# Nystromformer attention with a multiplicative feed-forward layer: the same pieces of work in another hand-planned order

## The chip, the cores and the metric

The kernel runs on one core of one Trainium2 chip. The metric is device time in microseconds (us) from launch to the last output byte. The chip's engines work side by side, each through its own instructions strictly in program order: TensorE (PE, with PEld for its weight loads), VectorE (DVE), ScalarE (ACT), GpSimd (POOL) and SyncE (SP). SP and POOL also start the transfers of this kernel, so a transfer that must wait holds back whatever its engine has queued behind it.

## The reference, cut to what matters

There are 8 batches of 8 heads with 576 rows of 64 numbers. `q_lm` and `k_lm` are means over groups of 18 rows, 32 of them per head.

```
A  = softmax(q @ k_lm.T / 8)         # 576 x 32
Bm = softmax(q_lm @ k_lm.T / 8)      # 32 x 32
C  = softmax(q_lm @ k.T / 8)         # 32 x 576
Z  = Bm.T / (norm1(Bm) * norminf(Bm) + 1e-6)
for _ in range(6): Z = 2*Z - Z @ Bm @ Z
attn = A @ Z @ C @ v                 # per batch and head
x    = attn, heads side by side      # 4608 x 512
out  = ((x @ w1) * (x @ w2)) @ w3 @ w_out
```

## The kernel before

All work is cut into small pieces, each a function call, and a long text `ORDER` lists the pieces by hand. The program walks the list once and every piece issues its instructions on its engines at that moment. There is no scheduler behind it: each engine's queue is the order of the list. A token is a letter for the kind of piece and digits for batch (or pair of batches), half and so on.

The first third of the time is the fold. Since nothing lies between the last two matrices, w3 and w_out are multiplied once into `w34`, in 112 pieces `f` (line 564) after a Strassen-like scheme. Its left factors come from 16 row blocks of w3, each loaded by a token `l` on SP's queue (line 525) and turned by a token `t` on PE (four transposes through the one PSUM tile `pst`, line 540), then copied out by ACT or, for every block of the kind "21", read by three DVE subtractions (lines 550 to 552). T1 to T4 are four DVE sums over w_out (line 510).

While this goes on, attention begins. These are its pieces:

- `K` loads q or k of a batch on POOL's queue (line 99, converting to 16 bits), `W` loads half of v of a batch on SP's queue (line 114).
- `T` is the DMA transpose of a loaded q or k, on SP's queue (line 122). It waits for the load, and for the attention of two batches earlier to be done with the two buffers `qT` or `kT`.
- `P` and `Q` are the same transposition made on PE instead, for two heads at a time (line 138), for k of batches 0 and 1 and q of batch 0. They go through PSUM tile `ptt`, which shares the one buffer with `pst`. `P` copies the result out on ACT, `Q` on DVE (line 139). The twelve such pieces are the only ones.
- `L` and `M` make the group sums, `L` on POOL in four instructions (lines 195 to 200), `M` on DVE in one (line 190). `X` and `Y` join the two halves of the sums into `lmk` and `qbd`: `X` with four copies on ACT and three sums on POOL (lines 208 to 215), `Y` with all of it on DVE.
- `C` and `c` are the scores for matrix C (PE line 304, ACT exponential line 309, row sums on POOL for `C` and on DVE for `c`). `V` and `v` are C @ v (line 332), `A` is the scores for matrix A (PE line 350, ACT line 355), `S` and `N` are their normalisation (lines 364 to 384).
- `B`, `J`, `R`, `I` and `Z` are, for a pair of batches, the scores Bm, a chain of twelve small DVE operations, the residual and the six steps of the inverse, and the product with C @ v.
- `G` and `g` multiply by w1 or w2 (line 414) with the result taken out by ACT (`G`, line 420) or DVE (`g`, line 422). `w` loads w1 or w2 on POOL's queue into the space of turned w3 blocks (line 612), `E` copies a part of it to the upper partitions on DVE (line 617).
- `U` is an eighth of a batch's two products: two PSUM tiles of `big`, the first copied out by ACT (line 441), the second multiplied with it by DVE (line 442). `D` multiplies 128 rows by w34 (line 463); ACT takes the result out (line 467) and SP stores it (line 483).

PSUM is what couples the engines most. During the fold there is one `big` tile, two of `small`, one of `pst` and three of `psw`. After the last `f` all of this is given back and there are three of `big` and two of `small`:

```
    def end_of_fold():
        psf.release()
        pf.release()
        ...
        ps["big"] = 3
```

Of the kernel before, what the change touches and what calls it, by code (L numbers as in the profile page):

```python
# [16 lines left out]
D = 64  # L17
# [19 lines left out]


ORDER = """
l f l f l f t f t f T1 f f f f t f f f t l l f f T2 f f f T3 f f l f l f f t f f f f W00 f f f T4 f f  # L40
Pk03 f f Pk02 t f f f f Pk01 f Pk00 f f Pq01 f f Pq02 Kk2 f Pq03 f Pq00 f W10 f Pk11 f Mq00 f Mk00 Pk12
Mk01 f Pk13 Mq01 f Kq2 f t f Pk10 X0 W01 f Mk10 f t f f f t f c01 f t c00 Tq1 Mq10 f w0 Lk11 W11 f A00 f
f f v01 A01 f f f Mq11 f f S0 f X1 f f Tq2 f B0 A10 f l J0 f C11 t f f f E3 f Tk2 Kk3 f f R0 f l v11 t
I00 f Lq20 Mk20 w1 l f t A11 I01 f v00 E0 f E2 C10 Mk21 t S1 E1 E7 I02 f f f f Tk3 f f W30 f f f E5 f
Lq21 Kq3 f Tq3 Kk4 f f v10 I03 Lk30 E4 f f f f f I04 f f X2 I05 f E6 Z0 f f W20 f f G110 g010 G000 C20
Kq4 N01 W21 N00 G011 g001 Mq30 Lq31 G100 C21 U U Mk31 G101 U X3 v20 N10 N11 U A21 B1 Tk4 U U A20 C31 Kk5
U Lk40 U v21 G111 W31 C30 Tq4 J1 D U R1 U Kq5 v31 I10 A30 A31 S2 Tk5 Lq40 W40 Lk41 Tq5 Mq41 U D N21 I11
S3 X4 Lk50 N20 U D I12 U I13 U I14 A41 D Kq6 C41 Mq50 U I15 Kk6 W41 A40 V30 U N30 D Lq51 N31 Z1 Mk51 Tq6
D X5 g210 G310 g200 D A51 B2 G201 Kk7 S4 G311 G211 J2 D U c40 D U A50 R2 U Tk6 Kq7 I20 U U I21 G300 U
I22 C50 W50 U U v41 Lq60 Lq61 g301 I23 Mk60 C51 Mk61 Tk7 D W51 Tq7 U U X6 D N41 D U U I24 A60 v40 S5 U U  # L50
Lk70 v50 W60 Mq70 I25 U c60 D U Lk71 Lq71 X7 N40 V51 D N50 C61 W70 Z2 A61 B3 D J3 G410 G400 G500 W71 D
N51 R3 W61 g501 G401 I30 g411 G510 I31 U I32 U C71 D U U v61 G511 I33 U U D c70 A70 I34 U U v70 S6 U D U
A71 I35 V71 U U V60 U Z3 D N61 U U G610 S7 G700 g600 D N60 U g601 G611 D U U G710 g711 U U U D N70 U
g701 U D U N71 D U U D U D U D U D U D U D U D D D D D
"""

@with_exitstack
# [690 lines left out]
```

## Time and profile before

| what | value |
|---|---|
| median of 13 runs | 288.23 us (284.05 to 296.13) |
| the profiled execution's own time | 285.41 us |
| its span | 283.2 us |
| PE busy | 267.4 us, 94% |
| DVE busy | 179.1 us, 63% |
| ACT busy | 140.5 us, 50% |
| POOL busy | 102.8 us, 36% |
| fold ends, three `big` begin | about 90 us |
| last DMA transpose issued, landed | 170.2 us, 177.2 us |

The own time is 2.2 us more than the span, for what lies around it. The median of the runs is 2.8 us above the profiled execution. A PE instruction's busy time counts from its start to a modelled end, so consecutive ones overlap; where below a piece's own length on PE is needed, it is taken from start to start of neighbouring pieces.

### The profile page before, as it was taken

What the parts mean: (1) busy time and instruction counts of PE and PEld (TensorE: products, weight loads), DVE (VectorE), ACT (ScalarE), POOL (GpSimd) and SP (SyncE); (2) the same over time, 40 slices, a digit from 0 to 9 for tenths busy, and PEclk for the clock granted to TensorE, in tenths of its full rate; (3) what the DMA queues carried; (4) which work ended last, traced back from release to release, by engine and by line L of the source; (5) the groups of instructions that cost most, each with busy time, mean ns of one, the idle gap of its engine ahead of it and who ended that gap; (6) DMA issues with size and microseconds to landing.
All of it is one profiled execution on the core that took longest, in us unless ns stands there. A gap on an engine that the chain in (4) does not pass through costs nothing.

```text
span 283.2 us, 8838 instructions
## 1 busy us (share of the span) xinstructions
PE 267.4 (94%) x3765; PEld 182.5 (64%) x3765; DVE 179.1 (63%) x341; ACT 140.5 (50%) x243; POOL 102.8 (36%) x148
## 2 busy tenths in 40 slices
PE   6999999997999899899999999999999999999994
PEld 2787766775885577566546766765767755665552
DVE  1766359897975877796677585959447586642310
ACT  2212356531322787455496655577565466443431
POOL 0170216276477666975540299750200000000000
PEclk9999999999999999999999999999999999999999
DMA  6999999999999997999999999539311012123344
GB/s 184 355 321 237 220 176 112 209 202 195 172 196 200 193 217 130 153 206 180 262 201 173 159 159 223 151 76 264 93 28 40 23 39 74 37 76 79 88 109 137
DMA packets 60999, 44.94 MB, mean 159 GB/s; under 512 B 32544, under 2 KB 53536, under 8 KB 60960
## 3 DMA queue, kind: packets, MB, share of 16 engines
q1 hardware_dynamic: 46112, 31.70, 50.6%
q0 software_dynamic: 13632, 11.54, 29.0%
q10 hardware_dynamic: 1216, 1.15, 1.3%
q8 instruction: 29, 0.48, 0.8%
q14 instruction: 10, 0.08, 0.1%
HBM read 38.80 MB, written 9.44 MB: 170 GB/s over the span
## 4 chain that ended last, share of the span: by engine, by line
PE 77%; ACT 7%; DVE 5%; DMA 4%; POOL 2%; SPq 2%; issue 2%; ACTq 0%; POOLq 0%; DVEq 0%
PE small L463 20%; PE big L435 19%; PE psw L564 14%; PE small L283 4%; PE small L332 4%; PE big L414 4%; PE pst L540 2%; PE big L304 2%; DMA raw<-in_moe_w_dram 2%; DMA w3g<-in_moe_w_dram 2%; PE ptt L138 1%; SPq L122 1%; PE big L350 1%; ACT gt L420 1%; PE big L381 1%
## 5 line engine op out<-in xcount | busy, mean ns | idle before, releaser
L442 DVE TENSOR_TENSOR ab<-a_sb,big 128x576 f16<-128x576 f16 x64 | 48.1, 753 | 44.8 <-ACT a_sb L441 40.7
L435 PE MATMUL big<-ahat,gt 128*128 128x288 f16 x512 | 71.3, 286 | 0.2
L463 PE MATMUL small<-w,ab 128*128 128x512 f16 (+1 forms) x296 | 67.5, 374 | 0.0
L435 PEld LDWEIGHTS <-gt 128*128 128x128 f16 x512 | 48.3, 98 | 18.3 <-issue 2.4
L441 ACT CAST a_sb<-big 128x576 f16<-128x576 f32 x64 | 40.9, 638 | 14.4 <-PE big L435 13.9
L463 PEld LDWEIGHTS <-ab 128*128 128x128 f16 x296 | 27.9, 98 | 29.0 <-issue 2.1
L467 ACT ACTIVATE o_sb<-small 128x512 f32<-128x512 f32 (+1 forms) x36 | 21.4, 594 | 36.9 <-PE small L463 36.9
L420 ACT ACTIVATE gt<-big 128x1024 f16<-128x1024 f32 x21 | 20.8, 1029 | 7.5 <-PE big L414 7.5
L314 POOL TENSOR_TENSOR e<-ect 96x384 f32<-96x384 f32 x11 | 10.9, 993 | 30.5 <-ACT ect L309 28.9
L414 PE MATMUL big<-wdup,zt 128*32 128x512 f16 x256 | 17.2, 381 | 1.4 <-DVE w L573 0.5
L341 ACT ACTIVATE xd<-small,rcr 128x64 f32<-128x64 f32 x16 | 5.0, 313 | 25.0 <-DVE rcr L339 25.0
L564 PE MATMUL psw<-wof,s 128*128 128x256 f32 x64 | 16.9, 392 | 0.0
L564 PE MATMUL psw<-tmat,s 128*128 128x256 f32 x64 | 16.5, 390 | 0.2 <-DVE tmat L510 0.2
L309 ACT ACTIVATE ect<-big 96x768 f32<-96x768 f32 x16 | 12.9, 806 | 6.0 <-PE big L304 5.9
L283 PE MATMUL small<-sz 32*32 32x64 f32 (+1 forms) x768 | 14.8, 214 | 0.5 <-DVE sz L271 0.5
L283 PEld LDWEIGHTS small<-sz 32*32 32x32 f32 x768 | 11.1, 105 | 6.3 <-issue 4.0
L384 DVE TENSOR_TENSOR ahat<-eat,big 128x576 f16<-128x576 f16 x16 | 11.9, 751 | 5.1 <-PE big L381 5.0
L564 PE MATMUL psw<-wof,a 128*128 128x256 f32 x48 | 14.4, 413 | 0.2 <-ACT a L547 0.2
L422 DVE TENSOR_SCALAR gt<-big 128x1024 f16<-128x1024 f32 x11 | 13.4, 1221 | 1.8 <-PE big L414 1.8
L332 PE MATMUL small<-vt,ect 96*32 96x64 f32 x768 | 14.0, 221 | 0.0
L355 ACT ACTIVATE eat<-big 128x576 f16<-128x576 f32 x16 | 10.3, 649 | 6.9 <-PE big L350 6.3
L564 PEld LDWEIGHTS psw<-tmat,s 128*128 128x128 f32 x64 | 11.4, 190 | 2.4 <-DVE tmat L510 0.6
(128 smaller groups left out, 398.7 us busy)
## 6 DMA issues: line engine op xcount, KB each, us to landing
vt<-in_v_dram SPq DMA_DIRECT2D x16, 576.0 KB, 6.4
out_dram<-o_sb SPq DMA_DIRECT2D x23, 192.0 KB, 2.3
nat<-in_k_dram POOLq DMA_DIRECT2D x7, 576.0 KB, 8.7
nat<-in_q_dram POOLq DMA_DIRECT2D x7, 576.0 KB, 7.8
raw<-in_moe_w_dram SPq DMA_DIRECT2D x13, 256.0 KB, 6.7
out_dram<-o_sb SPq DMA_DIRECT2D x24, 128.0 KB, 2.6
wdup<-in_moe_w_dram POOLq DMA_DIRECT2D x2, 1024.0 KB, 11.9
out_dram<-o_sb SPq DMA_DIRECT2D x23, 64.0 KB, 2.3
```

The source lines that it names most:

```text
L283: nc.tensor.matmul(psI[sl, 64 * a:64 * a + n], src[sl, a, 32:64], src[sl, a, 0:n], start=True, stop=True, tile_position=(32 * h, 32 * h))
L309: nc.scalar.activation(out=ect.rearrange("p (j a) h m -> p h j a m", a=2), in_=flat[0:P, 0:768].rearrange("p (h j a m) -> p h j a m", j=JJ ...
L332: nc.tensor.matmul(psV[32 * h:32 * h + 32, 0:64], st["ect", qd][:, c, h, :], st["v"][:, 4 * qd + h, c, :], start=(c == 0), stop=(c == TK - 1),
L414: nc.tensor.matmul(psG[32 * h:32 * h + 32, n, :], st["zt"][h % 2][:, qd, h // 2, :], wdup[w][:, 4 * qd + h, 512 * n:512 * n + 512], start= ...
L420: nc.scalar.activation(out=dst, in_=src, func=AXF.Copy, scale=1.0 / ZS)
L422: nc.vector.tensor_scalar(out=dst, in0=src, scalar1=1.0 / ZS, scalar2=None, op0=ALU.mult)
L435: nc.tensor.matmul(p[:, c, 0:HS], st["g", qd][:, w, 128 * j:128 * j + 128], st["ahat", qd][:, c, :], start=(qd == 0), stop=(qd == 1))
L441: nc.scalar.copy(out=a_sb, in_=p[:, :, 0:HS])
L442: nc.vector.tensor_tensor(out=ring["ab"][:, j, off:off + S].rearrange("p (c s) -> p c s", c=2), in0=a_sb, in1=pp[1][:, :, 0:HS], op=ALU.mult)
L463: nc.tensor.matmul(pso[:, f0:f1], ab[:, j, pos:pos + 128], w34[:, j, f0:f1], start=(j == 0), stop=(j == 7))
L467: nc.scalar.activation(out=o_sb[:, f0:f1], in_=pso[:, f0:f1], func=AXF.Copy, scale=1.0 / (X64 * X64))
L564: nc.tensor.matmul(ps_, lhs[:, 128 * c:128 * c + 128], right[:, c], start=(c == 0), stop=(c == 3))
```

## The change

Only the text `ORDER` changes. Before and after hold the same 486 pieces, and each token's work is the same but for the engine that some of them use: five of the twelve PE transpositions are copied out by DVE instead of ACT, sums move between DVE and POOL (15 pieces on POOL before, 17 after), 23 instead of 21 of the 32 `G`/`g` pieces use ACT, the exchange of batch 7 is on DVE instead of POOL, and five of the 16 `V`/`v` pieces change the place of their row sums (`V` takes them last). PE has the same instructions in another order. The order was found by a search in which the DMA transposes, and the loads of q and k of the later batches, are taken to land later than before.

```diff
 ORDER = """
-l f l f l f t f t f T1 f f f f t f f f t l l f f T2 f f f T3 f f l f l f f t f f f f W00 f f f T4 f f
-Pk03 f f Pk02 t f f f f Pk01 f Pk00 f f Pq01 f f Pq02 Kk2 f Pq03 f Pq00 f W10 f Pk11 f Mq00 f Mk00 Pk12
-Mk01 f Pk13 Mq01 f Kq2 f t f Pk10 X0 W01 f Mk10 f t f f f t f c01 f t c00 Tq1 Mq10 f w0 Lk11 W11 f A00 f
-f f v01 A01 f f f Mq11 f f S0 f X1 f f Tq2 f B0 A10 f l J0 f C11 t f f f E3 f Tk2 Kk3 f f R0 f l v11 t
-I00 f Lq20 Mk20 w1 l f t A11 I01 f v00 E0 f E2 C10 Mk21 t S1 E1 E7 I02 f f f f Tk3 f f W30 f f f E5 f
-Lq21 Kq3 f Tq3 Kk4 f f v10 I03 Lk30 E4 f f f f f I04 f f X2 I05 f E6 Z0 f f W20 f f G110 g010 G000 C20
-Kq4 N01 W21 N00 G011 g001 Mq30 Lq31 G100 C21 U U Mk31 G101 U X3 v20 N10 N11 U A21 B1 Tk4 U U A20 C31 Kk5
-U Lk40 U v21 G111 W31 C30 Tq4 J1 D U R1 U Kq5 v31 I10 A30 A31 S2 Tk5 Lq40 W40 Lk41 Tq5 Mq41 U D N21 I11
-S3 X4 Lk50 N20 U D I12 U I13 U I14 A41 D Kq6 C41 Mq50 U I15 Kk6 W41 A40 V30 U N30 D Lq51 N31 Z1 Mk51 Tq6
-D X5 g210 G310 g200 D A51 B2 G201 Kk7 S4 G311 G211 J2 D U c40 D U A50 R2 U Tk6 Kq7 I20 U U I21 G300 U
...
+f l t f W10 f f f f f t l f f f l f T1 f T2 t f l t f T3 f f f f f f f f t W00 f W01 f T4 f f l Qk03 f f
+t f f t f l f f l Pk02 f f f Qk00 f f Qk01 Kk2 f f Pq01 f f f Mk00 Pq02 Pq00 f Pk11 Qk10 f f Lk01 f Pq03
+Lq00 Kq2 f Mk10 f Mq01 f f Tq1 Pk12 f f X0 Qk13 f t t c00 f f w0 t Lk11 Lq10 f f c01 Mq11 f f f A01 A00
+X1 f f W11 v01 Tq2 l l l f t f B0 f J0 f f C11 f f f A11 f f Kk3 A10 S0 f R0 f f f t v11 w1 Mq20 Tk2 f f
+t Mk20 I00 f E0 f f t E2 v00 Mk21 C10 E1 Lq21 I01 f f f f f f f f S1 f Tk3 f E3 Kq3 X2 W30 E5 I02 Kk4 f
+f f f f f v10 I03 E6 f f f I04 f f f f E4 f Lk30 Tq3 f I05 E7 f Z0 f f f N00 G010 N01 G000 G011 Mk31
+g001 W20 Kq4 C20 C21 W21 N10 U A20 Mq30 G110 G100 g101 U U A21 V20 Mq31 Tk4 U N11 X3 U U S2 B1 C31 U U
+Kk5 Lk40 V21 A31 G111 A30 W31 Tq4 C30 J1 D R1 Tk5 W40 Kq5 U v31 Tq5 Mq40 I10 N20 D I11 U Lq41 U I12 S3 U
+D Lk41 U X4 D Lk50 Mk51 U Kq6 v30 I13 N31 A40 A41 I14 W41 N21 U I15 Lq50 U Kk6 Lq51 N30 D Z1 X5 D G200
+g210 g201 Tq6 D B2 G211 J2 G310 G311 D U W50 U R2 c40 c50 C41 Kk7 A51 I20 U U Tk6 Lq60 I21 U S4 G300 I22
...
 """
```

The five lines that follow in each list are left out here; they hold the products of batches 2 to 7 (`U`, `D`, `G`) with the last pieces of attention between them, and the last 17 tokens of both lists are the same `U` and `D`.

## The prediction

> **What bounds the kernel now.** First the page's busy shares, then the granted clock and the transfers over time.
>
> ```profile
> PE 267.4 (94%) x3765; PEld 182.5 (64%) x3765; DVE 179.1 (63%) x341; ACT 140.5 (50%) x243; POOL 102.8 (36%) x148
> ...
> PEclk9999999999999999999999999999999999999999
> DMA  6999999999999997999999999539311012123344
> ```
>
> PE is the bound, at full clock throughout, and transfers fill the first 180 us. Both orders hold the same 3765 matmuls, so I count a piece's work as its shortest start-to-start time in the trace (`f` 0.43, `t` 0.44, `P` 0.25, `I` 0.58, `U` 0.98, `D` 1.73 us and so on). Both lists then add up to 251.0 us of PE work. The rest of the 283.2 us span is 1.5 us before the first matmul, 3.9 after the last, and 27 us in which PE was late. Only those 27 can change. By stretches they are: 4.8 to 11.4 us (before the lists part), 1.0 to 24, 5.6 to 50, 0.7 to 58, 3.3 to 75, 1.5 to 90, 3.5 to 109, 1.5 to 119, 1.5 to 148 and 3.9 after that, the last mostly pieces a tenth over their shortest. I name a point by the PE work done before it, "w 41.7", and its time less w is the lateness there.
>
> Second, PE in order of time, where the largest late piece is:
>
> ```profile
> 65.41 0.66 PE L540 MATMUL pst<-ident,raw 128*128 128x128 f32 x4
> 66.53 0.65 PE L283 MATMUL small<-sz 32*32 32x64 f32 x32 [0.47 <-DVE sz L271]
> ...
> 67.64 0.59 PE L564 MATMUL psw<-wof,a 128*128 128x256 f32 x2
> 69.59 0.63 PE L540 MATMUL pst<-ident,w3g 128*128 128x128 f32 x4 [1.35 <-DMA w3g<-in_moe_w_dram]
> ```
>
> `t` number 14 waits for its w3 block. SP's own order tells why: the block's load stands behind two transposes.
>
> ```profile
> 54.15 5.76 SPq L122 DMA_TRANSPOSE qT<-nat  x1
> 59.97 0.57 SPq L525 DMA_DIRECT2D raw<-in_moe_w_dram  x1
> 60.63 3.44 SPq L122 DMA_TRANSPOSE kT<-nat  x1
> 64.12 1.05 SPq L525 DMA_DIRECT2D w3g<-in_moe_w_dram  x2
> ```
>
> Third, the waits of the PE transpositions, which share one PSUM buffer with `t`: each next user waits until the copy has ended.
>
> ```profile
> 27.56 0.42 PE L138 MATMUL ptt<-ident,nat 96*128 96x96 f16 x6
> 28.71 0.65 PE L540 MATMUL pst<-ident,raw 128*128 128x128 f32 x4 [0.73 <-ACT kT L139]
> ...
> 31.44 0.67 PE L564 MATMUL psw<-tmat,s 128*128 128x256 f32 x2
> 32.33 0.41 PE L138 MATMUL ptt<-ident,nat 96*128 96x96 f16 x6 [0.23 <-ACT kT L139]
> ```
>
> With no `f` between two users PE is 0.90 us late (28.71 less 27.56, less 0.25), with one 0.46, with two nothing.
>
> **The change part by part**, along the new list.
>
> *T1 and T2 now stand directly before the subtractions of `t` 5 on DVE.* That queue is then: a sum ending at 16.3, T1 and T2 (1.22 each), the first subtraction (0.69), so 19.4; the `f` that needs it is due at 18.4. 1.0 late against 0.33 (T2) before: +0.6.
>
> *The first transposition comes at w 16.80 instead of 18.96.* Its k load, gated as before, landed at 25.87; PE arrives at 16.80 + 7.2 (the lateness here before) + 0.6 = 24.6. Three v loads now go ahead of w3 loads on SP and compete with it. It can land in time (0), or where the first v load landed, 27.05 (+2.4). With the same landing it is 1.3; v puts less data than w3 between the shares of k, so I take +0.8. The late w3 blocks would land where v did, by 34.0, and are due after 45.
>
> *The one buffer.* Before: once 0.90, five times 0.46, and 1.2 around `t` 10, `t` 11 and c00, 4.4 in all. Now there is no `f` at Pq02–Pq00, Pk11–Qk10 and `t` 9–`t` 10 (2.7), one at Pq00–Pk11 and Qk13–`t` 9 (0.9), `t` 8 stands behind two DVE subtractions (0.85) and c00 behind X0 (0.4): 4.9, +0.5. The copies on DVE are not in this trace; by the nearest rows they lie between 0.31 us (a 144-wide cast from PSUM) and 0.75 (a 576-wide DVE product). I take 0.75, of the same width; the short end would give back 0.4.
>
> The Trainium skill (VectorE: DVE Perf Modes, "The perf-mode tier table") lets a copy of 16-bit data out of PSUM run at up to 2x. With the cycle counts of that page's section on the TRN2 errata (120 and half of 576, at 0.96 GHz) this makes an estimate of 0.43 us, and by it this item would be +0.2 instead of +0.5; no run here shows it yet.
>
> *A01 and A00 follow each other with one `big` tile.* The second waits for ACT's 0.65 us plus 0.2: +0.85, where `f` pieces hid it before.
>
> *B0 moves from w 44.96 to 41.70, but X1 does not get earlier.* POOL now does both Lk11 and Lq10 (3.1 each) after X0 (over at 47.6) and a 0.7 us load issue: 54.5. Four ACT copies behind A00's exponential end at 56.0, POOL's three sums (0.73, twice 0.76) at 58.3. PE arrives at 41.70 + 13.53 (lateness at B0 before) + 2.75 (so far) = 58.0: +0.35. At B0 the new order is 3.1 us behind.
>
> *The three `l` move ahead of Tk2.* `t` 13 and 14 are no longer late (E3, which held DVE before I00, moves too): I take out 0.68 + 1.51 = –2.2. The stall goes to Tk2. Tq2 is held by A00's exponential (54.4; its load, issued 3.4 later at 41.1, should land by 53.5). Then 5.8 for it and 1.7 for three loads: Tk2 issues at 61.9.
>
> ```profile
> DMA to landing us min/median/max: 5.7/6.9/10.4
> ```
>
> By that row for `kT` it lands at 68.8, at worst 72.3. Mk20 waits for it on DVE with I00's sum queued behind, and I01 waits for that sum. DVE is free at 70.2, Mk20 takes 1.35 and the sum 0.42, PE arrives at 71.9: +0.3 (2.4 at worst). Behind by 1.2.
>
> *The end of the fold.* The first new PSUM tile waits 2.5 us after Z0 for DVE's last sum; three `f` cover it instead of four: +0.43. Then follow seven `big` users with ACT's 1.03 us three times running and N00/N01 ahead. Counting slots with these rows, w 72.06 to 87.47 (15.4) takes 20.1 us; before, w 72.06 to 87.09 (15.0) took 18.5. +1.1 (0.5 to 1.6). R1 waits for J1's DVE chain in both (1.4): 0.
>
> *Batch 5's exchange.* X4 is 4.5 later in PE work and Lq50 is now on POOL, so Lq51 ends near 141.8 instead of 138.9 and X5's ACT copies hold D6 and G200: about 1.0 late against 0.6 at B2: +0.3.
>
> *After 150 us* the loads of batch 7 keep their slack: Kk7 slips some 7 us, but Tk7 waits for C51 in both orders. U6.2 (0.4 late) loses the DVE `g` before it: –0.5 with its neighbours.
>
> Sum: 0.6 + 0.8 + 0.5 + 0.85 + 0.35 – 2.2 + 0.3 + 0.43 + 1.1 + 0.3 – 0.5 = +2.5. Span 285.7, own time 285.41 + 2.5 = 287.9, and the median, 2.8 above it, 290.7.
>
> A rule speaks against the moved `E` copies. The row first:
>
> ```profile
> L617 DVE COPY wdup<-wdup x8: 681/689/1857, 64.0 to 87.8; 64x2048 f16<-64x2048 f16 x8
> ```
>
> The Trainium skill (SBUF — State Buffer, "SBUF: two separate sides") says that VectorE in a two-port mode and GpSimd lock each other out for a whole instruction, as the 1.86 fits. By the rule, an `E` between two `I` steps could cost one POOL operation, an estimate of 1 us more; by the median row nothing.
>
> **The rivals.** *Slower: Tk2 decides.* Transfers are saturated, and q2 is asked for 3.4 us later, so Tk2 may land at the slow end; from 70.2 each us of landing costs PE one, through Mk20 and I00's sum. For it: `t` 14's block also took long; against it: the loads before Tk2 are small. At 72.3 it adds 2.1: 292.8.
>
> *Faster: loads and copies come early.* The waits that I add before B0 and in the G stretch hang on landings and on copies queued behind others; if k0 lands in time and the DVE copies are at their short end, most have nothing to wait for, and what is left are –2.2 (w3 blocks), –0.5 (after 150 us) and –0.4 (the one buffer): 288.2 – 3.1 = 285.1. For it: `t` 13 and 14 show that transfers, not PSUM, made the largest lateness. Against it: A01–A00 and the G stretch need no transfer at all, and 27.56 to 28.71 shows the buffer's full price.
>
> *No effect.* Tq2 issues at 54.4 against 54.15, Tk7 and Tq7 stay, so waits only change places: 288.2.
>
> **How the numbers follow.** About 1% can be told from no change here, 2.9 us. My sum, 290.7, has 0.32, no effect 0.12: within 1% 0.44. Tk2 late, or k0 late at its 2.4 end: slower, 0.38. Faster 0.18. The range goes from 284.6 (the faster case less 0.5) to 294.4 (292.8 and the other 1.6 of the k load).
>
> **What would show it.** Right: no wait of PE for `w3g`; the first `ptt` late for `nat`; A00 0.85 after A01; B0 just after X1's `qbd`; Mk20 on DVE starting with Tk2's landing; span near 285.7. Wrong: U0.0 (96.2 before) earlier than 96, or lateness after 120 us that differs by over 1.5 us.

## The result and the profile after

| | order before | new order |
|---|---|---|
| median of the runs | 286.39 us (48 runs) | 291.39 us (11 runs, 287.09 to 293.48) |
| ratio, with its 95% interval | 1 | 1.0169 (1.0127 to 1.0211) |
| profiled execution: span | 283.2 us | 289.0 us |
| profiled execution: mean granted clock | 1.00 | 0.994 |

The new order is slower by 1.7%, some 4.8 us. These comparisons leave out runs that were disturbed. The mean clock says more: where it was 0.997 or higher, the median span was 283.7 us before (49 of 83 runs, over all that follows) and 286.5 us in the new order (7 of 18), a difference of 2.8; the lower clock was seen in 11 of 18 runs of the new order and in 34 of 83 before, too few to call it commoner.

The page of the new order, the rows that the prediction began with:

```profile
PE 270.2 (94%) x3765; PEld 183.3 (63%) x3765; DVE 179.8 (62%) x349; ACT 138.2 (48%) x236; POOL 106.1 (37%) x153
...
PEclk9998899999999999999999999999999999999999
DMA  6999999999999992999899989955901012122344
```

PE is still the bound, with the same 3765 matmuls, but in two slices near 30 us it did not have its full clock. PE in order of time there (start, duration, engine, line, tiles, and in brackets the idle time and what ended it):

```profile
22.64 1.24 PE L564 MATMUL psw<-wof,s 128*128 128x256 f32 x5
26.50 0.43 PE L138 MATMUL ptt<-ident,nat 96*128 96x96 f16 x6 [2.62 <-DMA nat<-in_k_dram]
26.77 1.71 PE L564 MATMUL psw<-wof,s 128*128 128x256 f32 x4
28.27 1.06 PE L540 MATMUL pst<-ident,raw 128*128 128x128 f32 x4
```

PE waits 2.62 us for k of batch 0. Then two `f` take 1.71 us and a `t` 1.06; the prediction counts 0.43 and 0.44 us a piece. The busy times by stretches show why (columns: stretch, length, busy PE, PEld, DVE, ACT and POOL with their numbers of instructions, granted clock, DMA share, GB/s):

```profile
23.70:27.11 3.41, 0.79 (x9) 0.59 (x9) 1.08 (x2) 0.00 (x0) 0.00 (x0) 1.00 1.18 240
27.11:30.52 3.41, 3.41 (x12) 2.66 (x10) 2.15 (x5) 0.00 (x0) 0.00 (x0) 0.50 1.19 251
30.52:33.93 3.41, 3.41 (x23) 2.79 (x22) 1.23 (x3) 1.22 (x2) 0.00 (x0) 1.00 1.25 242
```

In the stretch with the wait PE was busy for 0.79 of 3.41 us; for the next 3.41 us it had half its clock.

The largest late piece of the order before was `t` 14, which waited for its w3 block. The same lines of SP and PE now:

```profile
55.86 3.40 SPq L122 DMA_TRANSPOSE qT<-nat  x1
59.31 0.57 SPq L525 DMA_DIRECT2D raw<-in_moe_w_dram  x1
59.93 1.81 SPq L525 DMA_DIRECT2D w3g<-in_moe_w_dram  x2
61.83 4.08 SPq L122 DMA_TRANSPOSE kT<-nat  x1
...
69.41 0.60 PE L540 MATMUL pst<-ident,w3g 128*128 128x128 f32 x4
71.92 0.60 PE L540 MATMUL pst<-ident,w3g 128*128 128x128 f32 x4
```

The blocks are asked for ahead of Tk2, and neither `t` on `w3g` has a wait in brackets.

I use one measure for the rest: the lateness of PE that the prediction defines, and how much it grows between pieces (`f24` is the 24th `f` of the list). "Again" is a second profile of the unchanged new order (the first experiment below), "k0 apart" the second experiment.

| stretch | before | new | again | k0 apart | predicted change | new less before | again less before |
|---|---|---|---|---|---|---|---|
| launch to f24 | 7.18 | 6.92 | 8.04 | 7.13 | +0.6 | -0.26 | +0.86 |
| f24 to f32 | 0.21 | 4.72 | 3.71 | 0.83 | +0.8 and `t` 8's 0.85 | +4.51 | +3.50 |
| f32 to f60 | 5.33 | 4.47 | 4.47 | 5.11 | rest of the buffer's, -0.35 | -0.86 | -0.86 |
| f60 to f76 | 0.83 | 2.16 | 2.15 | 2.17 | +1.2 | +1.33 | +1.32 |
| f76 to f88 | 3.29 | 0.76 | 0.77 | 0.76 | -1.9 | -2.53 | -2.52 |
| f88 to R1 | 6.50 | 8.31 | 8.31 | 8.29 | +1.53 | +1.81 | +1.81 |
| R1 to U2.0 | 1.54 | 2.85 | 1.35 | 1.35 | +0.3 | +1.31 | -0.19 |
| U2.0 to the last piece | 4.14 | 4.52 | 4.52 | 4.53 | -0.5 | +0.38 | +0.38 |
| sum | 29.02 | 34.71 | 33.32 | 30.17 | +2.5 | +5.7 | +4.3 |

The launch row says little of the order. PE begins at 1.46 us in every profile of this document, but an `f` then takes 0.86 us instead of 0.43 until the clock is first recorded at full, which is 5.4 to 13.4 us into the profile (10.9 in the order before, where the prediction took the clock to be full throughout). With that moment the lateness at f24 goes from 5.8 us (full at 5.9) to 8.7 (full at 13.4).

Behind the launch two rows differ between the two profiles of the same order, f24 to f32 and R1 to U2.0. In the first profile they are also the two that the prediction missed most.

### The profile page after: what moved, and what is told of

The parts are those of the page before. It is cut to its first block, busy times and chain, and to the rows that moved or that the text cites. A ratio compares the mean times of both kernels' runs of the same rounds, so it can differ in the third digit from the quotient of the medians.

```text
span 289.0 us, 8843 instructions
## 1 busy us (share of the span) xinstructions
PE 270.2 (94%) x3765; PEld 183.3 (63%) x3765; DVE 179.8 (62%) x349; ACT 138.2 (48%) x236; POOL 106.1 (37%) x153
## 4 chain that ended last, share of the span: by engine, by line
PE 74%; DMA 11%; ACT 4%; DVE 4%; POOL 3%; issue 2%; ACTq 0%; DVEq 0%; POOLq 0%
PE big L435 20%; PE small L463 19%; PE psw L564 12%; DMA nat<-in_k_dram 5%; PE big L414 4%; PE small L332 4%; PE small L283 4%; DMA wof<-in_moe_w_out_dram 4%; PE big L304 3%; DMA qT<-nat 2%; ACT gt L420 1%; PE pst L540 1%; PE big L381 1%; PE ptt L138 1%; PE big L350 1%
## 5 line engine op out<-in xcount | busy, mean ns | idle before, releaser
L314 POOL TENSOR_TENSOR e<-ect 96x384 f32<-96x384 f32 x11 | 10.9, 994 | 48.8 <-ACT ect L309 32.7
L420 ACT ACTIVATE gt<-big 128x1024 f16<-128x1024 f32 x23 | 22.6, 1022 | 6.0 <-PE big L414 5.9
L564 PE MATMUL psw<-wof,s 128*128 128x256 f32 x64 | 19.3, 423 | 0.0
L547 ACT COPY a<-pst 128x512 f32<-128x512 f32 x9 | 5.3, 584 | 24.7 <-PE pst L540 24.6
L564 PE MATMUL psw<-wof,a 128*128 128x256 f32 x48 | 13.0, 399 | 0.0
L211 POOL TENSOR_TENSOR lmk<-lp,lx 128x256 f16<-128x256 f32 x7 | 5.1, 730 | 21.0 <-ACT lx L209 21.0
L422 DVE TENSOR_SCALAR gt<-big 128x1024 f16<-128x1024 f32 x9 | 10.9, 1220 | 3.1 <-PE big L414 1.8
```

The lines of the kernel that those rows point to most:

```text
L420: nc.scalar.activation(out=dst, in_=src, func=AXF.Copy, scale=1.0 / ZS)
L564: nc.tensor.matmul(ps_, lhs[:, 128 * c:128 * c + 128], right[:, c], start=(c == 0), stop=(c == 3))
```

## The experiments

Ratios are to the order before, with 95% intervals. Each edit is a piece of `ORDER`, cut to the tokens that move.

### The new order again

No edit.

> The new order itself, unchanged, a second time. The traces so far cut time into stretches of 3.41 us on a grid that lies differently in each run; each half-clock stretch followed a stretch in which PE was busy for 0.52 of the time or less (0.23 before 26.5 us in the first profile of this order; 0.54 and 0.63 elsewhere were followed by full clock). Theory: the PE wait for k0 of about 2.6 us lies wholly in one such stretch in most runs and is split in some; so most runs show a mean clock of 0.994 or less, some 0.997 or more, and these are 2 to 3 us shorter. The lateness between f24 and the end, without a half-clock stretch, is about 26 us against 21.8 in the kernel before. Rival: the clock in the first profile was an accident of that run; then most runs are at 0.997 or more and the median is near 287.

Ratio 1.0156 (1.0087 to 1.0226). The clock was 0.991 to 0.994 in four of six runs, spans 287.6 to 287.9, and 0.997 in two, 285.6 and 286.1: 2 us shorter, as the theory has it. The runs of the result part less cleanly: 285.1 to 290.6 us at 0.997 and more, 288.3 to 291.5 below. In this profile PE waited for k0 just as long (2.63 us), but the grid of 3.41 us cut the wait in two (same columns):

```profile
22.50:25.91 3.41, 2.50 (x14) 1.87 (x12) 1.98 (x3) 0.58 (x1) 0.45 (x1) 1.00 1.19 240
25.91:29.33 3.42, 1.69 (x15) 1.54 (x16) 1.18 (x3) 0.00 (x0) 0.00 (x0) 1.00 1.18 245
29.33:32.74 3.41, 2.78 (x17) 2.11 (x16) 2.34 (x5) 0.59 (x1) 0.00 (x0) 1.00 1.22 267
```

The clock stayed at 1.00, and f24 to f32 cost 3.71 us instead of 4.72. So half clock cost 1.0 us of the first profile. (This run also had half clock from 8.8 to 12.2 us, which is in the launch row.) Lateness from f24 to the end grew by 25.3 us, 21.8 before: the change is 3.4 us without any half-clock stretch behind f24.

### k of batch 0: the first transposition later, the v loads back, PE kept busy

One piece later:

```diff
-f l Qk03 f f t f f t f l f f l Pk02 f f f Qk00
+f l f f t f f t f l f Qk03 f f l Pk02 f f Qk00
```

> The new order with one piece moved: Qk03, the first transposition of batch 0's k, stands six `f` and two `t` later (3.5 us of PE work), the rest is as it was. Theory: the 2.6 us for which PE waited for k0's load at 26.50, and the 4.5 us at a granted clock of 0.62 that followed it (pieces of 0.43 us took 0.85), cost 4.3 us, and no later wait takes them back. PE then reaches Qk03 near 27.3, after the landing near 26.5; no PE wait for `nat`, granted clock 1.00 from 26 to 31 us, lateness at f32 near 0 against the kernel before instead of 4.26, and the span 4 us shorter than the new order's 289.0, about 285; ratio to the kernel before near 1.00. Rival: the pieces behind are held by landings (w3 blocks, q2, the batch 1 loads), so that being earlier at f32 only lets PE wait there; then the lateness is back before B0 or at Mk20, and the span is 288 to 289.

Ratio 1.0101 (1.0040 to 1.0161), span 284.5. The wait is gone and the clock here at 1.00:

```profile
26.89 0.63 PE L540 MATMUL pst<-ident,raw 128*128 128x128 f32 x4 [0.63 <-issue]
27.35 0.60 PE L564 MATMUL psw<-wof,s 128*128 128x256 f32 x2
27.79 0.59 PE L564 MATMUL psw<-tmat,a 128*128 128x256 f32 x2
28.24 0.41 PE L138 MATMUL ptt<-ident,nat 96*128 96x96 f16 x6
```

The theory holds for the wait: from f24 to f32 lateness grows by 0.83 us, 2.9 less than in the second profile of the new order, and 2.2 of these are still there at the end (23.0 against 25.3 us from f24). The 0.83 is `t` 8 behind its DVE subtractions. The rest of the new order, taken without this wait, is 1.2 us slower than the order before (23.0 against 21.8), so the ratio near 1.00 that was expected is not reached.

The three v loads behind three of the `l` again:

```diff
-f l t f W10 f f f ... t W00 f W01 f T4 f f l Qk03 f f t f f t f l f f l Pk02
+f l t f f f f ... t f f T4 f f l Qk03 f f t f f t f l f f l W00 W10 W01 Pk02
```

> The new order with the three v loads W10, W00 and W01 put back behind three of the `l` loads on SP (after the `l` ahead of Pk02); nothing else moves. Theory: k0's load, issued at 11.8 us, landed 14.65 us after its issue in the new order and 12.97 in the one before because the v loads ahead of it share the transfers; without them it lands near 24.8 to 25, PE, there at 23.9, waits about 1 us, and the granted clock stays at 1.00 or falls for a shorter time. Lateness at f32 2.5 to 3.3 us smaller, span about 286. Rival: it is the load of k0 itself, its 12 to 15 us set by the w3 loads that were put in front, and the v loads only trade places with them: landing still 26 to 26.5 us, the wait 2 to 2.6 us, span 288.5 to 289.5.

Ratio 1.0039 (0.9995 to 1.0083), span 284.3, clock 1.00. k0 landed 12.3 us after its issue, at 23.80, and PE waited 1.08 us for it. Over all profiles the split is clean: with the v loads ahead, k0 takes 14.1 to 15.8 us from issue to landing (ten profiles), without them 12.1 to 13.0 (four: this one, the order before, and the two below that change the order before). The v loads are the cause of some 2 us of the landing, and the rival falls. This profile had full clock from 5.9 us on (the first of the new order from 10.0), and f24 came 1.1 us earlier, so its span flatters it.

Dummy matmuls ahead of Qk03:

```diff
-f l Qk03
+f l H Qk03        # H: six matmuls of zeros, 512 columns, into a small tile
```

> The new order with six dummy matmuls (512 columns of zeros, 0.42 us each) put on PE directly before Qk03, into an unused PSUM tile; they add 2.5 us of work just where PE waited 2.6 us for k0. Nothing else moves. Theory: the clock of 0.62 from 26.5 to 31 us follows from PE's pause, not from k0's lateness; with PE busy up to the landing, Qk03 starts at 26.5 as before, but the pieces behind it take 0.43 us again, granted clock 1.00 from 26.5 to 31, and about 1.9 us of the 4.26 us of lateness at f32 are gone: span near 287. Rival 1: the clock falls at that place for another cause (the number of matmuls so far, the transposition itself): the pieces still take 0.85 and the span is 289. Rival 2: the pieces behind were slow because of transfers or copies, not the clock: then the granted clock reads 1.00 and they take 0.85.

Ratio 1.0077 (1.0019 to 1.0135). It did not tell what it should. At full clock a dummy took 0.22 us, not the 0.43 of the same matmul at the launch, where PE has half its clock, and k0 came at 28.56 in this run, so PE still waited 3.09 us. The clock was then halved for 6.8 us, two stretches, though PE was busy 2.67 of the first 3.41 us. The second profile of the new order answered the question instead.

### The w3 loads ahead of Tk2, alone

```diff
-Tq2 f B0 A10 f l J0 ... R0 f l v11 ... Mk20 w1 l f t
+Tq2 l l l f B0 A10 f J0 ... R0 f v11 ... Mk20 w1 f t
```

> The order before with one part of the change: three `l` loads stand directly behind Tq2, ahead of Tk2 (before, they stood at J0, behind R0 and behind w1). Theory: of the new order's parts this one alone gains: `t` 13 and `t` 14 no longer wait for their w3 blocks (0.68 and 1.51 us), Tk2's transposition comes about 1.7 us later on SP and lands near 68 to 69, where I00 to I02 wait for DVE's Mk20 up to 0.6 us; span 1.5 to 2.2 us under the kernel before's, ratio 0.993 to 0.995. Rival: Mk20 takes over the place of the w3 blocks: DVE's sum waits for Tk2, I00 and I01 behind it, and the gain is 0 to 0.5 us; a further rival, that the lateness is slack that the fold's end gives back, shows as a lower lateness at S1 and the same one at Z0.

Ratio 1.0018 (0.9972 to 1.0065): no gain. This run's timeline, DVE and PE:

```profile
71.70 1.35 DVE L190 TENSOR_REDUCE lp<-kT 128x128 f32<-128x1152 f16 x1 [3.49 <-DMA kT<-nat]
72.97 0.68 DVE L550 TENSOR_TENSOR s<-pst,a 128x512 f32<-128x512 f32 x1
74.30 1.11 PE L540 MATMUL pst<-ident,w3g 128*128 128x128 f32 x4 [2.15 <-DVE s L551]
```

`t` 14 no longer waits for its block, but DVE stands 3.49 us before Mk20, for Tk2, which landed 9.5 us after its issue; the subtractions of `t` 14 are behind it, and `t` 15 needs them. That is the rival, in a worse place than I01. From f76 to f88 lateness grew by 5.5 us, 1.7 of it at most from a half-clock stretch that followed at 74.2. In the new order the same loads gain 2.5 us, because there DVE comes to Mk20 about 4 us later, at 72.1 instead of 68.2, and Tk2, which landed at 68.17, is not waited for.

### B0: A00 apart from A01, and one sum on DVE

Three edits together, Qk03 as above and:

```diff
-A01 A00 X1 f f W11     ... Lq50
+A01 f f A00 X1 W11     ... Mq50
```

> The new order with three repairs together: Qk03 six `f` and two `t` later, batch 5's first q sums on DVE, and two `f` between A01 and A00, which share one `big` tile. Theory: the three places that made the new order slower are independent and add up: 4 us at k0, 1.2 at batch 5, and 0.8 at A00, of which B0 may take a part back because its operands come later than PE; span 283 to 284, ratio to the kernel before 0.99 to 1.00. If the rest of the gain (w3 blocks ahead of Tk2, 1.9 us) is kept too, it is level with the kernel before or just faster. Rival: repairs overlap, a later landing decides in each case, and the sum is 2 us short: span 286.

Ratio 1.0073 (1.0033 to 1.0112). A00's wait of 0.85 us disappears, and from f60 to f76 PE loses 2.2 us as in the new order: 0.61 at v01, for the sums of c01 on DVE, the rest in pieces of 0.2 and less. Its profile, with a span of 289.0, also had half clock from 40.0 us and the late q5 that is told below. The next kernel takes X1's operands earlier (the two `f` and Qk03 as above, batch 5 not):

```diff
-Lk11 Lq10 ... W11 v01 Tq2 l l l f t f B0
+Lk11 Mq10 ... W11 Tq2 l l l f t f v01 B0
```

> The new order with Qk03 six `f` and two `t` later, and at B0: two `f` between A01 and A00, batch 1's first q sums on DVE instead of POOL, and v01 behind the next `f t f`. Theory: with the waits at A00 taken apart alone, the same time was lost again at v01 (0.61 us for DVE's e sums) and at B0, because X1 on POOL came late behind two sums of 3.1 us; with one of the two on DVE, X1 ends about 3 us earlier, B0 waits for nothing, and from f60 to f76 PE loses 1.0 us or less instead of 2.17. Span 283 to 284 in a run without a half-clock stretch, 1.0 to 1.3 us less than with Qk03 moved alone. Rival: DVE, where Mq10 now stands ahead of c01's sums and Mq11, is the one that decides: `t` 11 and c01 wait, and f60 to f76 still loses about 2.

Ratio 1.0132 (1.0065 to 1.0199); f60 to f76 2.1 us. The rival holds, in one chain of this run's timeline, DVE, ACT and PE:

```profile
52.05 1.33 DVE L190 TENSOR_REDUCE lp<-qT 128x128 f32<-128x1152 f16 x1
53.31 0.54 DVE L314 TENSOR_TENSOR e<-ect 96x384 f32<-96x384 f32 x1
...
54.41 1.34 DVE L190 TENSOR_REDUCE lp<-qT 128x128 f32<-128x1152 f16 x1
...
55.84 0.40 ACT L208 COPY lx<-lp 64x256 f32<-64x256 f32 x1 [0.39 <-DVE lp L190]
...
57.09 0.22 PE L226 MATMUL small<-lmk,qbd 64*32 64x32 f16 x8 [0.62 <-POOL qbd L215]
```

The lines at 52.05 and 54.41 are Mq10 and Mq11, with c01's sums between them. POOL is free at 51.7 now, but ACT's copies of the q sums wait for Mq11, and B0 waits for the `qbd` made from them. The work that left POOL came back in DVE's queue.

### R1 behind one more U

On top of the last edits:

```diff
-J1 D R1 Tk5 W40 Kq5 U v31
+J1 D Tk5 W40 Kq5 U R1 v31
```

> As the last one, and R1 behind the next U piece instead of directly behind D. Theory: the 1.4 us for which PE waits at R1 for J1's DVE chain, in the order before as in the new one, is covered by the 0.98 us of U; the wait falls to about 0.45 and the span by 1.0 us, to 282 to 283 in a run without a half-clock stretch: level with or just under the kernel before's. Rival: J1's chain is held by DVE's products for that U, and R1's subtraction on DVE now comes behind Mq40, so that I10 waits instead: no gain.

Ratio 1.0160 (1.0057 to 1.0262). Its profiled execution had half clock from 40.0 and from 152.7 us and a meeting of q5 and k5, so its span says nothing; from U0.4 to R1, at full clock, lateness grew by 2.0 us instead of 3.0: the theory holds in that stretch. The next kernel's timeline of PE, with R1 in the same place, has the same 2.0:

```profile
114.78 1.14 PE L435 MATMUL big<-ahat,gt 128*128 128x288 f16 x8
116.21 0.45 PE L269 MATMUL small<-btn,bt 32*32 32x32 f32 x32 [0.29 <-DVE btn L259]
```

Why J1's chain is late shows in its two products on DVE, `bm` (line 251) and `btn` (line 259). In the profiles each takes 0.29 us in all 44 cases where no instruction of POOL runs beside it, and 0.39 us or more in 67 of the 68 others. In J1 they run beside POOL's work, k5's load and sums of k4 for `bm` and C30's sums for `btn`, and take 1.31 and 0.82 us in the order before, 1.16 and 0.83 in the new one: together 1.4 to 1.6 us more, as much as R1's wait. No run moves that work of POOL away.

### The one PSUM buffer, spaced out

On top of that:

```diff
-Pq01 f f f Mk00 Pq02 Pq00 f Pk11 Qk10 f f Lk01 f Pq03 ... f Mk10 f Mq01 f f Tq1 Pk12
+Pq01 f f Mk00 Pq02 f f Pq00 f f Pk11 f f Qk10 f f Lk01 Pq03 ... f Mk10 Mq01 Tq1 Pk12
```

> As the last one, and with two `f` between the neighbours of the one PSUM buffer `pst` around Pq02, Pq00, Pk11 and Qk10 (the same eleven `f`, spread evenly). Theory: the waits after Pq02 (0.90), f44 (0.46) and Pk11 (0.89) vanish and nothing that comes later is due before PE reaches it; lateness at f60 falls by 1.5 to 2.2 us, span by the same, to 280.5 to 281.5: under both kernels. Rival: X0 and c00, or the landing of batch 1's q, decide the time at which the stretch ends; then t9 or c00 waits by as much more and the gain is under 0.5 us.

Ratio 1.0067 (1.0014 to 1.0120), span 284.2. The three waits vanish, 2.25 us in all, and from f24 to f60 lateness still grows by 6.2 us (5.9 with only Qk03 moved):

```profile
34.51 0.43 PE L138 MATMUL ptt<-ident,nat 96*128 96x96 f16 x6 [1.23 <-DMA nat<-in_q_dram]
41.61 0.42 PE L138 MATMUL ptt<-ident,gt 96*128 96x96 f16 x6 [0.23 <-ACT qT L139]
44.78 0.66 PE L540 MATMUL pst<-ident,raw 128*128 128x128 f32 x4 [1.07 <-DVE kT L139]
```

PE waits 1.23 us for q0's landing, 0.39 with only Qk03 moved. That wait lies ahead of the three that vanished, so they cannot have covered it; q0 landed at 34.46 us instead of 33.49. Behind it 0.46 us comes back at Pk12 and 1.0 at `t` 9, which waits for Qk13's copy: that stands on DVE behind the sums Mk10 and Mq01 (1.34 us each) and ends at 44.7 us, 44.4 with only Qk03 moved. So q0 apart, 0.6 us is won. The rival is right that `t` 9 then waits; it is DVE's queue that decides, not X0 or a landing. What the spacing may save is the clock: with these waits close together half clock followed them in three of nine profiles, and in neither of the two spaced ones.

### Batch 5's exchange

The first profile's timeline there, SP, POOL, ACT and PE:

```profile
120.03 3.22 SPq L122 DMA_TRANSPOSE kT<-nat  x1
120.08 0.79 POOL L99 DMA_DIRECT2D nat<-in_q_dram  x1
...
134.49 2.78 SPq L122 DMA_TRANSPOSE qT<-nat  x1
...
146.84 0.40 ACT L208 COPY lx<-lp 64x256 f32<-64x256 f32 x1 [2.41 <-POOL lp L200]
148.35 0.27 PE L226 MATMUL small<-lmk,qbd 64*32 64x32 f16 x16 [0.94 <-ACT o_sb L467]
149.26 1.48 PE L414 MATMUL big<-wdup,zt 128*32 128x512 f16 x24 [0.64 <-ACT gt L420]
```

q5's load, issued at 120.08, landed at 134.42, so its transposition is issued at 134.49; X5's copies on ACT wait for POOL's sums, and behind them stand D6's copy and G200's. Is it POOL or the load?

```diff
-N21 U I15 Lq50 U
+N21 U I15 Mq50 U
```

> The new order with one change: the sums of q of batch 5's first half are on DVE (as in the order before) and no longer on POOL. Theory: POOL's two sums one behind the other (3.1 us each, behind a load issue), ending at 146.8, held ACT's exchange copies, and those held D6's store copy and G200; without the first, Lq51 ends near 143.5, the PE waits of 0.94 and 0.64 us near 148 and 149 are gone or under 0.3, and the lateness that was added between Z1 and B2 goes from 1.3 to about 0.1; span about 287.8, 1.2 us less than the 289.0 of the new order. Rival: the exchange is late because q5's transposition by DMA landed at 140.0 us instead of 130.5; then DVE's sum starts no earlier, holds the DVE queue for 1.35 us in its place, and the span is 288.5 to 289.5.

Ratio 1.0133 (1.0083 to 1.0184). The PE waits are gone, R1 to U2.0 takes 1.28 us. But it takes 1.35 with Lq50 on POOL in the second profile of the new order and with Qk03 moved: q5 had landed 6 to 7 us earlier in all three (127.3 to 128.2). And where q5 was late again with its first sum on DVE (the kernel with three repairs), PE lost more, 3.3 us. That kernel's timeline, DVE and PE:

```profile
140.99 1.35 DVE L190 TENSOR_REDUCE lp<-qT 128x128 f32<-128x1152 f16 x1 [1.89 <-DMA qT<-nat]
142.26 0.74 DVE L442 TENSOR_TENSOR ab<-a_sb,big 128x576 f16<-128x576 f16 x1
143.06 0.39 PE L463 MATMUL small<-w,ab 128*128 128x512 f16 x1 [1.95 <-DVE ab L442]
```

DVE waits for q5's transposition, the product of a `U` stands behind it, and a `D` needs that product. So it is the load, whichever engine makes the sum. The fourteen profiles of both orders and all edits, by the issue of k5's transposition less the issue of q5's load:

```
gap, us          q5's load, issue to landing, us
+2.49 to +2.36   6.8  6.9  8.2
+1.13 to +0.23   7.2  7.5  8.0  8.0
+0.06 to  0.00   10.2  10.6  11.1
-0.03 to -0.05   14.3  14.9  15.4
-0.60            9.9
```

Before, k5's load landed 8.2 us after its issue and the gap was 2.36. In the new order it lands 5.8 us after, just when POOL has done the sums that stand between the two loads (5.95 and 5.98 us from issue to issue in the first profiles of the two orders). So they meet by a hair. One more run moves q5's load ahead of those of the sums that come last:

```diff
-Tq4 C30 J1 D Tk5 W40 Kq5 U R1
+Tq4 Kq5 C30 J1 D Tk5 W40 U R1
```

> The last kernel with spaced `pst` pieces, and q5's load on POOL put ahead of C30's e sums, so that it is issued about 2.2 us earlier. In the traces so far q5's load and k5's transposition by DMA were issued within 0.06 us of each other six times, and q5 then landed 10.2 to 15.4 us after its issue; where the load went 0.2 us or more ahead it took 6.9 to 8.0. Theory: it is this meeting that made batch 5's exchange late; with the load 2.2 us ahead it lands 6.5 to 8 us after its issue, q5's transposition is issued near 123 to 125 instead of 128 to 135, and between Z1 and U2.0 PE loses 0.5 us or less; span 283.5 to 284. Rival: k5's landing and the load behind it keep their distance because the load's start is set elsewhere, or the long landing is a matter of the traffic then: q5 still takes 10 us or more.

Ratio 1.0061 (1.0022 to 1.0100), span 286.3. The gap is 2.38, q5 lands 8.2 us after its issue, its transposition is issued at 125.63, and from Z1 to U2.0 PE loses 0.7 us: the theory holds for the landing, but PE lost no more than that where q5 landed at 127 to 128 us, so nothing is won by a still earlier one. The span was lost in two places. Tk2 landed 10.6 us after its issue, and lateness from f76 to f84 grew by 2.3 us instead of 0.8. And R1 waited 1.17 us instead of 0.29, which is the edit's own doing (this run's timeline, POOL and DVE; the last line from the kernel without the edit):

```profile
116.65 0.79 POOL L99 DMA_DIRECT2D nat<-in_q_dram  x1
116.91 1.70 DVE L259 TENSOR_TENSOR btn<-bt,rn 128x128 f32<-128x128 f32 x1
...
115.34 0.82 DVE L259 TENSOR_TENSOR btn<-bt,rn 128x128 f32<-128x128 f32 x1
```

The moved load now runs beside J1's last product but one, and C30's sum behind it too, and the product takes 1.70 us.

### The order before with R1 behind two U

The edit that gained by itself, on the order before:

```diff
-J1 D U R1 U Kq5 v31
+J1 D U U R1 Kq5 v31
```

> The order before with one edit: R1 behind two U pieces instead of one. Theory, from the new order's run with R1 behind a U (its PE wait there fell from 1.43 to 0.46 us): the 1.4 us for which PE waits at R1 for J1's DVE chain are covered by the 0.98 us of the second U, nothing else moves, and the span is 0.9 to 1.0 us shorter, near 282.2 with a clock of 1.00: faster than both kernels by a third of a per cent or more. Rival: the second U's product on DVE now stands ahead of R1's subtraction, and I10 or the next U's waits by as much: lateness at Z1 as before, no gain.

Ratio 0.9970 (0.9927 to 1.0013). From U0.4 to R1 lateness grew by 1.0 us instead of 2.0. The profiled span, 289.5, has half clock from 131.0 and a wait of 3.4 us behind I12 and says nothing; the median span of the runs at a clock of 0.997 and more is 282.9 (6 runs), 283.7 in the runs of the order before beside it. The sign is as expected and the size too, but the interval contains 1: no version is shown to beat the order before, and of the edits of the new order the one with the v loads back comes nearest, at 1.0039.

## Why the prediction was right, and where it was wrong

The forecast of 290.7 us came near 291.4, and the direction was right, but the nearness is luck: two errors met. The sum of steps said +2.5 us and the comparison says +4.8; and the base, 288.23 for the order before, came out at 286.39 when more runs were there. Point by point:

**T1 and T2 (+0.6): about right.** From f4 to f24 lateness grew by 0.92 us before and 1.27 in the new order, +0.35. The launch row also holds when the clock became full, which the prediction had not seen and which moves f24 by up to 3 us between profiles.

**The first transposition (+0.8): the step that failed.** It cost 2.9 us, and in the first profile half clock added 1.0. The prediction took k0 with the same landing or that of the first v load, 0 to 2.4 us late, and chose +0.8 because v was to put less data between the shares of k. Both ends were off: PE was there at 23.9 us, not 24.6, and k0, issued 1.1 us earlier, landed at 26.45, 14.6 us after its issue instead of 13.0. The v loads ahead cost it some 2 us; with them moved back it lands at 23.80. That a wait also halves the clock after it was in no step.

**The one buffer (+0.5): too high.** Its waits add up to 4.6 us in the second profile, 4.4 before: +0.2. The page of the Trainium skill (VectorE: DVE Perf Modes, "The perf-mode tier table") let the prediction estimate 0.43 us for the DVE copy, and +0.2 by it. The new order's profile has these copies in its view by tile (min/median/max in ns):

```profile
L139 DVE COPY kT<-ptt x5: 444/458/459, 27.0 to 47.0; 128x576 f16<-128x576 f16 x5
```

0.46 us, near the estimate and nearer to the short one of the two rows than to the 0.75 that I took. And the spaced version shows that of 2.25 us of these waits most comes back at DVE's queue.

**A01–A00 and B0 (+1.2): right in sum, +1.3.** A00 came 0.84 late, but B0 only 0.1; the rest lies in pieces of 0.2 and less. And A00's wait is no cost by itself: taken apart, it comes back at v01 (0.61, for sums on DVE), and with v01 moved too at B0 (0.62, for X1's `qbd`).

**The w3 loads (-2.2 and +0.3): right, -2.5.** `t` 14 had no wait for `w3g`. The sign that Mk20 would start with Tk2's landing was wrong: it began 3.9 us later, behind `t` 14's subtractions, so Tk2 cost nothing. The `E` copies, against which the prediction named a rule, took 1.44 us at most, and no piece from f76 to f88 is late by more than 0.13. The rival "Tk2 decides" is what happened in the order before with the same three loads moved, where DVE is earlier, and it cost 1.5 us in the last kernel of the new order, where Tk2 landed at 71.3 instead of 68.2.

**The fold's end and the G stretch (+0.43 and +1.1): right, a little low**, +1.8 in three profiles. (The slots as the prediction counts them give +1.2, not +1.1.) No run takes this cost apart. R1's wait was equal in both, as said, and 1.0 of its 1.4 us could be covered.

**Batch 5 (+0.3): mechanism right, size a matter of chance.** -0.2 or +1.3, by whether two transfers meet.

**After 150 us (-0.5): wrong sign, +0.4** in three profiles. The late `U` did lose its 0.4 us, but six other pieces (D11, G610, G611, U6.4, G711 and U7.1) are about 0.2 late each; no run tries them.

Of the two signs against it, U0.0 began at 98.5 us, not ahead of 96; that lateness after 120 us should differ by no more than 1.5 us failed by a little in the first profile (1.3 from R1 to U2.0 and 0.4 after it) and held in the second (0.2 in all). Between the rivals: "loads and copies come early" fell with k0, "no effect" with all of the above. What the new order won, 2.5 us at the w3 blocks, it had lost to the v loads put ahead on the same queue some 45 us earlier.

## What to carry to other kernels

A load put ahead of others on one queue can delay what lands on another queue (here k0, by some 2 us): before moving one, list what is due in the next 15 us and give each the later end of its landing times. A wait on the engine that bounds the kernel can cost more than its length once it empties most of a 3.4 us stretch (2.62 us cost 1.0 more here), so such waits are better spread than collected. And a wait that goes away is a gain only if what comes next has slack; here A00's wait and the PSUM buffer's each uncovered DVE's queue, and the w3 blocks, in the order before, the landing of Tk2.

## What the runs showed of the hardware

**Clock.** Behind the launch all half-clock stretches are 3.41 us or twice that, on a grid that lies differently in each run. PE's busy share (union of its records) in the 3.41 us before them, and of the emptiest stretches that were followed by full clock, between 20 and 270 us:

```
followed by half clock: 0.21 0.23 0.26 0.31 0.31 0.40 0.51 0.52 0.54
followed by full clock: 0.46 0.49 0.54 0.62 0.63 and more
```

The two rows overlap. They part if the 16-bit transpositions of `P` and `Q` (line 138) are not counted as busy: then the first row is 0.13 to 0.40 and the second 0.41 and more. So these pieces seem to do little to keep the clock up, which would also be why the three highest of the first row (0.51, 0.52, 0.54) lie where they stand closest; no run tests it. (From half clock a stretch with 0.78 was followed by half clock once more, in the run with the dummies.)

The Trainium skill (TensorE: Matmul & The Clock Gate, "What's actually happening") has the free-running window of 3413 ns, which agrees. Its rule against idle gaps over about 3.4 us ("HAM oscillation — how this bites in real kernels") is too mild here: 2.62 us in one gap did it, and in one run a stretch with no PE wait over 0.9 us (the 0.52).

**Transfers.** Where q5's load and k5's DMA transposition were issued within 0.06 us of each other both were slow: 10.2 to 15.4 us for the load instead of 6.8 to 8.2 (9.9 once, with the transposition 0.60 us ahead), and 10.9 to 13.4 us for the transposition instead of 6.6 to 10.1. The 0.06 is no limit: in the profile of the order before with R1 later, k4's transposition went 1.52 us ahead of q4's load, and both took 13.1 us. What in the transfer engines does it no run here shows.
